# Routing by expert number, a two-column table ahead of the first gathers, and the last scatters behind the branch

## The chip, the cores and the metric

One core of a Trainium2 chip runs the whole program in one launch. The metric is device time in microseconds: 544.03 us is the median of three runs of the kernel before (543.95 to 544.78). The profile is one more execution.

## The reference

Two layers in a row, on 2048 tokens of width 512, all in f32:

```
x  = q                                                   # 2048 x 512
h  = x + q' * (longconv(shift(k) * v) + D * ...)         # q' = layernorm(x)
z  = layernorm(h);  logits = z @ w_gate                  # 8 experts
e  = argmax(logits)  (first on a tie);  gate = softmax over one value
out = h + gate * (silu(z @ w1[e]) @ w2[e])               # F = 1792
```

Each token goes through one expert. The change touches only what lies between the logits and the first expert's first matmul, and the last stores.

## The kernel before

**Stages.** The convolution (a planner, `Plan`, writes each engine's order from costs and due times) fills `h_dram`, 2048 rows of 516 words: 512 of h, then mean, 1/deviation, and the gate in two words. It ends at about 182 us. Then comes the routing, written by hand in program order (L614 to L727), then a branch on `wide_i`, and inside it the experts (`experts(caps)`, L730 to L943), one after another, smallest first.

**Order.** In the routing and the experts every engine runs its instructions in the order in which the program lists them, SP and POOL included; between engines there are only semaphores. An engine that waits holds back all that is listed behind.

**Routing.** A token of partition p and column j (NJ = 16 columns) gets a one-hot row `oh` over experts (L621 to L636) and its place within its expert from a running sum and two matmuls (`incl`, `pn`, `pr`). Experts are ranked by load: `key` (L652), `gt`, `sr` (L657, L660). The place word is rank times 4096 plus place (L668 to L674), cut into column `col_i` and row `lo_f`. The token table, 128 rows by 24 columns (three per expert, in rank order), is a sum of 16 matmuls of one-hot rows `ohlo` (L686, one VectorE instruction per j, 128 x 128) with marked tokens `vt` (L679, L682): `ptab`. From it come `idxg` (gather rows, L694) and `idxs` (scatter rows, L719 to L722).

**First loads.** Two indirect gathers (L707) bring the rows of the first expert's two tiles into `first`; SP loads the first two weight chunks (L715), once it has read the expert's number from `perm_i`. The gathers read `h_dram`, whose last columns are stored by L649. Matmuls `keep_warm` on constants (L605) fill waits on TensorE.

**Branch.** Each engine loads `wide_i` into a register (L947) and branches (L948) to one of three copies of `experts`; these inputs take the copy with the caps SNUG (the first expert has 240 rows, tiles of 128 and 112).

**Experts.** Weights come in 512 KB chunks, 14 per expert (7 for w1, 7 for w2). ScalarE rounds a chunk to `whi`, VectorE takes `wlo = raw - whi` (`split`, L800). Rows are normalised (`norm`, L763), transposed and split into `xh`, `xl` (`turn_x`, L775). `up` (L810) makes 12 matmuls per 128 columns of F, in the order whi.xh, wlo.xh, whi.xl; then ScalarE's Silu (`s`, three buffers), VectorE's `hh`, POOL's `hl`. Loads of chunks 2 to 5 are held back by a write into their tile behind the first `norm` (L797). `store` and `send` (L854) scale by the gate, add h and scatter rows to the output. The last expert's rows leave by three scatters: one of tile 0, two of half-width for tile 1.

## Time and profile before

| | |
|---|---|
| median of 3 runs | 544.03 us |
| the profiled execution | 544.39 us, span 542.5 us |
| TensorE | busy 519.1 us (96%), granted clock 0.991 |
| VectorE, ScalarE, POOL | 75%, 49%, 48% |
| DMA | 105.26 MB, 194 GB/s in the mean |
| convolution, to the last logits | 0 to about 182 us |
| routing, to the first expert matmul | about 182 to 198.6 us |
| experts | 198.6 to about 534.8 us |
| last scatter, landing, end | 534.8 to 542.5 us |

Times below are microseconds from the start of the span. The execution takes 1.9 us more than its span, and lies 0.36 us above the median of the runs.

### The profile page before, as it was taken

What the parts mean: (1) busy time and instruction counts of PE and PEld (TensorE: products, weight loads), DVE (VectorE), ACT (ScalarE), POOL (GpSimd) and SP (SyncE); (2) the same over time, 40 slices, a digit from 0 to 9 for tenths busy, and PEclk for the clock granted to TensorE, in tenths of its full rate; (3) what the DMA queues carried; (4) which work ended last, traced back from release to release, by engine and by line L of the source; (5) the groups of instructions that cost most, each with busy time, mean ns of one, the idle gap of its engine ahead of it and who ended that gap; (6) DMA issues with size and microseconds to landing.
All of it is one profiled execution on the core that took longest, in us unless ns stands there. A gap on an engine that the chain in (4) does not pass through costs nothing. (4 is left out here: it accounts for less than half of the span.)

```text
span 542.5 us, 12152 instructions
## 1 busy us (share of the span) xinstructions
PE 519.1 (96%) x4812; PEld 451.9 (83%) x4812; DVE 405.6 (75%) x558; ACT 265.1 (49%) x410; POOL 260.7 (48%) x297
## 2 busy tenths in 40 slices
PE   9999989999998699999999999999999999999994
PEld 9867767767656469789999999999988988988973
DVE  3779899898997968859855784974884784785851
ACT  2697887544320346545435445545543644554520
POOL 0555659865641136618503921840760760851832
PEclk9999999999999989999999999999999999999998
DMA  8918786659661278674654665674676566576401
GB/s 285 380 55 261 236 276 195 179 153 287 187 170 43 60 263 320 218 256 166 199 182 140 204 199 166 189 259 141 206 219 233 180 210 231 194 219 205 155 2 41
DMA packets 42468, 105.26 MB, mean 194 GB/s; under 512 B 6480, under 2 KB 14800, under 8 KB 42018
## 3 DMA queue, kind: packets, MB, share of 16 engines
q1 hardware_dynamic: 39602, 95.89, 54.9%
q0 software_dynamic: 2800, 8.51, 4.9%
q8 instruction: 40, 0.66, 0.5%
q14 instruction: 26, 0.21, 0.1%
HBM read 95.96 MB, written 8.47 MB: 193 GB/s over the span
## 5 line engine op out<-in xcount | busy, mean ns | idle before, releaser
L826 POOL TENSOR_TENSOR hl<-s,hh 128x240 fp32r<-128x240 f32 (+5 forms) x112 | 114.4, 1035 | 162.2 <-DVE hh L825 161.7
L807 DVE TENSOR_TENSOR wlo<-raw,whi 128x1024 fp32r<-128x1024 f32 x112 | 160.5, 1443 | 38.8 <-ACT whi L806 35.2
L806 ACT ACTIVATE whi<-raw 128x1024 fp32r<-128x1024 f32 x112 | 114.6, 1051 | 3.5 <-DMA raw<-in_w_dram 3.5
L824 ACT ACTIVATE s<-acc 128x240 f32<-128x240 f32 (+5 forms) x112 | 43.1, 387 | 98.1 <-PE acc L821 63.4
L825 DVE CAST hh<-s 128x240 fp32r<-128x240 f32 (+5 forms) x112 | 55.0, 501 | 30.1 <-ACT s L824 29.9
L821 PE MATMUL acc<-xh,whi 128*128 128x240 f32 (+5 forms) x448 | 73.0, 285 | 0.1
L821 PE MATMUL acc<-xh,wlo 128*128 128x240 f32 (+5 forms) x448 | 72.0, 283 | 0.0
L821 PE MATMUL acc<-xl,whi 128*128 128x240 f32 (+5 forms) x448 | 71.9, 283 | 0.0
L821 PEld LDWEIGHTS acc<-xh,whi 128*128 128x128 f32 x448 | 61.7, 189 | 0.8 <-ACT xh L782 0.3
L821 PEld LDWEIGHTS acc<-xl,whi 128*128 128x128 f32 x448 | 61.6, 189 | 0.0
L821 PEld LDWEIGHTS acc<-xh,wlo 128*128 128x128 f32 x448 | 61.4, 189 | 0.0
L842 PE MATMUL acc<-whi,hh 128*128 128x512 f32 (+2 forms) x136 | 54.3, 399 | 0.0
L842 PE MATMUL acc<-whi,hl 128*128 128x512 f32 (+2 forms) x136 | 53.6, 394 | 0.0
L842 PE MATMUL acc<-wlo,hh 128*128 128x512 f32 (+2 forms) x136 | 53.5, 394 | 0.0
L265 POOL TENSOR_TENSOR acc<-acc,ac 128x512 f32<-128x512 f32 x26 | 33.1, 1280 | 37.1 <-ACT acc L253 19.2
L845 PE MATMUL acc<-hh,whi 128*128 128x304 f32 (+2 forms) x168 | 49.8, 296 | 0.0
L845 PE MATMUL acc<-hl,whi 128*128 128x304 f32 (+2 forms) x168 | 49.2, 293 | 0.0
L845 PE MATMUL acc<-hh,wlo 128*128 128x304 f32 (+2 forms) x168 | 49.1, 292 | 0.0
L296 ACT ACTIVATE st<-pa 128x512 f32<-128x512 f32 x64 | 37.3, 595 | 20.6 <-PE pa L293 20.3
L293 PEld LDWEIGHTS pa<-kv,tw 128*128 128x128 f32 x256 | 30.2, 191 | 12.2 <-ACT st L296 8.7
L293 PE MATMUL pa<-kv,tw 128*128 128x128 f32 x256 | 33.5, 282 | 2.2 <-ACT st L296 2.2
L782 ACT ACTIVATE xh<-pt 128x512 fp32r<-128x512 f32 (+5 forms) x18 | 9.6, 535 | 53.1 <-PE pt L781 53.1
(171 smaller groups left out, 878.2 us busy)
## 6 DMA issues: line engine op xcount, KB each, us to landing
raw<-in_w_dram SPq DMA_DIRECT2D x112, 512.0 KB
tv<-in_tab_v_dram SPq DMA_DIRECT2D x12, 512.0 KB
h<-in_q_dram SPq DMA_DIRECT2D x16, 256.0 KB
kt<-in_kt_dram SPq DMA_DIRECT2D x3, 1216.0 KB
v<-in_v_dram SPq DMA_DIRECT2D x12, 256.0 KB
kern<-in_ssm_dram SPq DMA_DIRECT2D x12, 256.0 KB
h<-in_x_dram SPq DMA_DIRECT2D x12, 256.0 KB
h_dram<-h SPq DMA_DIRECT2D x12, 256.0 KB
```

The costliest lines, as they stand in the source:

```text
L265: nc.gpsimd.tensor_add(T[a, c, u], T[a, c, u], T[b, c, u])
L293: nc.tensor.matmul(p[:, :, j], tw[:, u * UJ + j, r, :], src[:, j, :], start=True, stop=True)
L296: nc.scalar.activation(T["s" + kind, c][:, r * NU + u], T["pa", kind, c, u, r], AF.Copy)
L782: nc.scalar.activation(xh[:, at, r0:r0 + m], pt[:, :, :m], AF.Copy)
L806: nc.scalar.activation(whi, raw, AF.Copy)
L807: nc.vector.tensor_sub(wlo, raw, whi.bitcast(F32))
L821: nc.tensor.matmul(pu, a[:, k, fs], b[:, k, :], start=i == 0, stop=i == 3 * ND - 1)
L824: nc.scalar.activation(s, pu, AF.Silu)
L825: nc.vector.tensor_copy(hh[:, f, :], s)
L826: nc.gpsimd.tensor_sub(hl[:, f, :], s, hh[:, f, :].bitcast(F32))
L842: nc.tensor.matmul(pd[:ds_.stop - ds_.start], b[:, f, ds_], a[:, f % 2, :], start=f == 0 and i == 0, stop=f == last - 1 and i == 2)
L845: nc.tensor.matmul(pd, a[:, f % 2, ds_], b[:, f, :], start=f == 0 and i == 0, stop=f == 2 * NCH - 1 and i == 2)
```

## The change

In the routing, places are counted by expert number, not by rank: a constant matmul adds 32 x 128 times the expert (`base_b`, made early on POOL) to `pr`. The place words, tables and one-hots become 16-bit integers or f16 with j innermost. The least loaded expert is found as the minimum of `key` (`least`); two columns (`m0`, `ptab0`, `idx0`) are made for it alone ahead of all else, with the one-hots in two instructions (j 0 to 8, 9 to 15) in place of 16. Then follow the branch flags, the table of 24 columns (`m24`), the ranking, and `perm_i`; the reordering of the table by rank (`other_tables`) goes behind the branch.

The store of mean and 1/deviation is issued behind the reciprocal, with zeros for the gate; the gate (`gated`) is stored later, by SP behind the load of chunk 5, and the first expert's rows are gathered a second time for their gate, in the up stage. `least` in place of `perm_i` gives SP the first expert.

In the first expert both first chunks are rounded ahead of the norms, `wlo` of chunk 0 comes in two halves, and the two column groups of chunk 0 take turns by factor. The last expert's three results are written to tiles `ends`, and the three scatters stand behind the join of the branches.

```
+    sb("kt", "places")                    # 16-bit tables in the buffer of kt, which now stays
...
+    nc.gpsimd.tensor_scalar(base_b, const("e")...[P, E, NJ], 32.0, None, op0=ALU.mult)
+    nc.gpsimd.tensor_copy(tile_b, const("tile")...[P, 24, NJ])
+    nc.gpsimd.tensor_copy(iota_b, const("iota")...[P, P, NJ])
...
+    nc.tensor.matmul(pr, one_b, base_b, start=True, stop=False)
-    keep_warm(5, 128)
+    keep_warm(8, 128)
...
-    nc.vector.reciprocal(rec[:, :, 1], rec[:, :, 1])
     nc.vector.scalar_tensor_tensor(cand, ...)
+    nc.vector.reciprocal(rec[:, :, 1], rec[:, :, 1])
+    nc.sync.dma_start(h_rows[:, :, D:RW], rec)
...
-    keep_warm(5, 128)
-    nc.vector.reciprocal(rec[:, :, 2], rec[:, :, 3])
-    nc.gpsimd.tensor_mul(rec[:, :, 2], rec[:, :, 2], rec[:, :, 3])
-    nc.sync.dma_start(h_rows[:, :, D:RW], rec)
+    keep_warm(8, 128)
     nc.vector.scalar_tensor_tensor(key, pn, float(E), const("e"), ...)
+    nc.vector.tensor_reduce(least, key, axis=AX.X, op=ALU.min)
+    nc.vector.tensor_scalar(least, least, E - 1, None, op0=ALU.bitwise_and)
+    for t in range(2):
+        nc.gpsimd.tensor_scalar(tile0[:, t], least.to_broadcast([P, NJ]), 32.0, float(t), ...)
...
+    r2, c_i, col_i, lo_i                  # 4 VectorE instructions; lo_i is a bitwise and
+    m0 = marks("m0", tile0, 2)            # is_equal, then times tok_b: 128 x 32 each
+    for js in (range(0, 9), range(9, NJ)):
+        nc.vector.tensor_tensor(ohlo[:, :, at], iota_b[:, :, at], lo_i[:, at]..., op=ALU.is_equal)
+        for j in js:
+            nc.tensor.matmul(ptab0, ohlo[:, :, j], m0[:, :, j], ...)
+    keep_warm(2, 512)
+    nc.vector.tensor_scalar(idx0, ptab0, -1.0, 0.0, op0=ALU.add, op1=ALU.max)
+    over, nover, nover, wide_i            # as before, now behind idx0
+    m24 = marks("m24", tile_b, 24)        # 128 x 384 each
+    for j in range(NJ):
+        nc.tensor.matmul(ptab, ohlo[:, :, j], m24[:, :, j], ...)
+    keep_warm(2, 448)                     # before: keep_warm(4, 432)
+    nc.scalar.activation(tabs_e..., ptab, AF.Copy)
     gt, sr, eqm, eqe, perm_i              # moved here, all on VectorE
+    nc.vector.reciprocal(gated[:, :, 0], gated[:, :, 1])
     for t in range(2):
         nc.gpsimd.indirect_dma_start(out=rows0[t], ..., in_offset=... idx0[:, t:t + 1])
+    nc.gpsimd.tensor_mul(gated[:, :, 0], gated[:, :, 0], gated[:, :, 1])
-    place0 = nc.sync.value_load(perm_i[0:1, ORDER[0]:ORDER[0] + 1], ...)
+    place0 = nc.sync.value_load(least[0:1], ...)
...
+    def other_tables():                   # 3 VectorE, then 6 small POOL instructions
...
+        for s in range(len(raw0)):
             load_w(s)
+            split_hi(s)                   # whi of chunks 0 and 1
+        norm(0, *firsts[0])
+        split_lo(0, 0, 512)
         for s in range(len(raw0), AHEAD):
             load_w(s, s < 6)
+            if s == 5:
+                nc.sync.dma_start(h_rows[:, :, D + 2:RW], gated)
+        norm(0, *last, 0); norm(0, *last, 1); split_lo(0, 512, 1024)
+        turn_x of all tiles; split_lo(1); other_tables(); split(2); split(3)
...
+                for fs in ([0, 1],) if s == 0 else ([2 * r], [2 * r + 1]):
+                    up(n, fs, whi, wlo)
+                if n == 0 and 2 <= r < 2 + len(tiles(0)):
+                    gather(0, r - 2)
...
+    scatter(out, idxs[:, end - 1:end], ends[0], S)       # behind the Else arm
+    for i in range(2):
+        scatter(halves, half_i[:, i:i + 1], ends[i + 1], 2 * S)
```

## Rows read from the trace of the kernel before

**Rows 1.** Busy time by stage (window; its length; busy us and count of TensorE's matmuls, its weight loads, VectorE, ScalarE, POOL; granted clock; DMA share; GB/s).

```profile
187.00:200.00 13.00, 9.95 (x43) 6.04 (x44) 8.99 (x37) 3.77 (x9) 5.43 (x9) 0.74 0.65 185
...
260.00:500.00 240.00, 240.00 (x1738) 227.38 (x1738) 167.56 (x194) 114.85 (x180) 106.20 (x102) 1.00 0.62 200
```

**Rows 2.** VectorE in order of time, in the routing (start, duration of the merged group, engine, line, operation, output and input, count).

```profile
183.48 0.26 DVE L627 RECIPROCAL rec<-rec 128x16 f32<-128x16 f32 x1
183.65 0.23 DVE L629 SCALAR_TENSOR_TENSOR cand<-eq,cs 128x128 f32<-128x128 f32 x1
...
185.33 0.17 DVE L652 SCALAR_TENSOR_TENSOR key<-pn,cs 128x8 f32<-128x8 f32 x1
...
187.52 0.55 DVE L679 TENSOR_TENSOR ohhi<-tile_b,col_i 128x384 f16<-128x384 bf16 x1
187.99 3.32 DVE L686 TENSOR_SCALAR ohlo_f<-iota_b,lo_f 128x128 f16<-128x128 f16 x16
191.22 0.27 DVE L691 TENSOR_TENSOR over<-key,rungs 1x128 f32<-1x128 f32 x1
...
191.73 0.16 DVE L694 TENSOR_SCALAR idxg<-pt 128x24 int32<-128x24 f32 x1
...
192.04 0.16 DVE L697 TENSOR_REDUCE wide_i<-nover 1x2 int32<-1x16 f32 x1
```

**Rows 3.** SP's queue and POOL in order of time: the store of the last columns of `h_dram`, the first weight loads, the first two gathers.

```profile
185.61 0.61 SPq L649 DMA_DIRECT2D h_dram<-rec  x1
188.62 0.94 SPq L715 DMA_DIRECT2D raw<-in_w_dram  x2
...
192.20 1.20 POOL L707 DMA_INDIRECT first<-h_dram,idxg  x1 [3.22 <-DVE wide_i L697]
193.71 0.95 POOL L707 DMA_INDIRECT first<-h_dram,idxg  x1 [0.30 <-issue]
```

**Rows 4.** POOL's sequencer on the line of the gathers: four waits for DMA queues, from the first, which ends when the store of L649 has landed, to the last (duration min/median/max in ns, then first and last start).

```profile
L707 POOLq EVENT_SEMAPHORE  x4: 17/43/43, 190.8 to 191.1; - x4
```

**Rows 5.** From the branch to the first expert matmul: the register loads ahead of the branch on VectorE and ScalarE, then ScalarE, VectorE and TensorE in order of time.

```profile
L947 ACTq TENSOR_LOAD <-wide_i x1: 466/466/466, 192.2 to 192.2; - x1
...
193.52 1.06 ACT L806 ACTIVATE whi<-raw 128x1024 fp32r<-128x1024 f32 x1 [1.40 <-DMA raw<-in_w_dram]
197.17 0.60 ACT L782 ACTIVATE xh<-pt 128x512 fp32r<-128x512 f32 x1 [2.59 <-PE pt L781]
198.15 0.69 ACT L782 ACTIVATE xh<-acc 128x224 fp32r<-128x224 f32 x2 [0.38 <-PE acc L781]
...
195.82 0.55 DVE L772 TENSOR_SCALAR xr<-first 128x512 f32<-128x512 f32 x1
...
197.24 0.74 DVE L772 TENSOR_SCALAR xr<-first 112x256 f32<-112x256 f32 x2 [0.84 <-DMA first<-h_dram,idxg]
...
198.56 0.82 PE L821 MATMUL acc<-xh,whi 128*128 128x240 f32 x4
```

**Rows 6.** TensorE in order of time (matmuls of the tables and of `keep_warm`), and last the stretch in which its granted clock was at half (columns as in rows 1).

```profile
182.50 1.48 PE L607 MATMUL warm<-cs 128*128 128x128 f32 x10
...
189.03 2.53 PE L687 MATMUL pt<-vt,ohlo_f 128*128 128x24 f16 x16 [2.25 <-DVE ohlo_f L686]
191.41 4.77 PE L607 MATMUL warm<-cs 128*128 128x432 f32 x8
...
187.87:194.70 6.83, 5.67 (x21) 3.37 (x22) 4.29 (x23) 1.25 (x2) 2.99 (x3) 0.50 0.57 170
```

**Rows 7.** VectorE's groups by line and form between 182 and 200 us (count, busy us, mean ns of one): two inputs of f32 at 1024 and 512 elements per partition, one input at 512 and 256.

```profile
L807 DVE TENSOR_TENSOR wlo<-raw,whi 128x1024 fp32r<-128x1024 f32 x2 | 2.5, 1225 | 3.0 <-ACT whi L806 3.0
L772 DVE TENSOR_SCALAR xr<-first 112x256 f32<-112x256 f32 x2 | 0.7, 410 | 0.8 <-DMA first<-h_dram,idxg 0.8
...
L783 DVE TENSOR_TENSOR xl<-pt,xh 128x512 fp32r<-128x512 f32 x1 | 0.7, 682 | 0.0
...
L772 DVE TENSOR_SCALAR xr<-first 128x512 f32<-128x512 f32 x1 | 0.5, 546 | 0.0
```

**Rows 8.** POOL in the up stage of the first expert, and ScalarE's Silu that waits for it.

```profile
214.42 2.35 POOL L826 TENSOR_TENSOR hl<-s,hh 128x240 fp32r<-128x240 f32 x2 [0.23 <-DVE hh L825]
216.94 1.08 POOL L759 DMA_INDIRECT hr<-h_dram,idxg  x1 [0.17 <-issue]
...
215.16 0.37 ACT L824 ACTIVATE s<-acc 128x240 f32<-128x240 f32 x1 [0.55 <-POOL hl L826]
...
217.62 0.40 PE L842 MATMUL acc<-whi,hh 128*128 128x512 f32 x1
```

**Rows 9.** The end: POOL's last work in order of time, its branch out of the arm, and the drains of POOL and of SP at the end (ns min/median/max, first and last start).

```profile
518.21 2.35 POOL L826 TENSOR_TENSOR hl<-s,hh 128x240 fp32r<-128x240 f32 x2 [0.22 <-DVE hh L825]
533.03 1.00 POOL L857 DMA_INDIRECT out_dram<-o,idxs  x1 [12.47 <-DVE o L856]
...
535.61 0.95 POOL L857 DMA_INDIRECT out_dram<-o,half_i  x1 [0.30 <-POOLq L948]
...
L948 POOLq COMPARE_BRANCH  x1: 46/46/46, 535.4 to 535.4; - x1
...
L1119 POOLq DRAIN  x1: 3311/3311/3311, 538.3 to 538.3; - x1
...
L1119 SPq DRAIN  x2: 7/10/13, 540.4 to 540.5; - x2
```

More of the change, by code (lines that the diff above doesn't have):

```diff
@@ L153 @@
     oh = keep.tile([P, E, NJ], BF16, name="oh")
-    tile_b = keep.tile([P, 24], BF16, name="tile_b")
     tok_b = keep.tile([P, NJ], F16, name="tok_b")
-    c_i = keep.tile([P, NJ], I32, name="c_i")
-    col_i = keep.tile([P, NJ], I32, name="col_i")
-    lo_f = keep.tile([P, NJ], F32, name="lo_f")
+    gated = keep.tile([P, NJ, 2], F32, name="gated")
+    c_i = keep.tile([P, NJ], I16, name="c_i")
+    col_i = keep.tile([P, NJ], I16, name="col_i")
+    lo_i = keep.tile([P, NJ], I16, name="lo_i")
     perm_i = keep.tile([1, E], I32, name="perm_i")
@@ L164 @@
     idxs = keep.tile([P, 24], I32, name="idxs")
-    iota_b = keep.tile([P, P], F16, name="iota_b")
+    idx0 = keep.tile([P, 2], I32, name="idx0")
     tri_b = keep.tile([P, P], BF16, name="tri_b")
@@ L435, in casts @@
             nc.gpsimd.tensor_scalar_add(rungs[:, 0, i], rungs[:, 1, i], 8.0 * (SNUG[i] - TIGHT[i]))
-        for a, n in ((iota_b, "iota"), (tri_b, "tri"), (one_b, "one"), (tile_b, "tile")):
+        for a, n in ((tri_b, "tri"), (one_b, "one")):
             nc.gpsimd.tensor_copy(a, const(n))
@@ L598 @@
     plan.run(PACE, ZERO, AHEAD)
+    sb("kt", "places")
+    place_f = T["places"].rearrange("p a b -> p (a b)")
+    place_h = place_f.bitcast(I16)
+    iota_b = place_h[:, :P * NJ].rearrange("p (m j) -> p m j", j=NJ)
+    tile_b = place_h[:, P * NJ:(P + 24) * NJ].rearrange("p (c j) -> p c j", j=NJ)
+    tile0 = place_h[:, (P + 24) * NJ:(P + 26) * NJ].rearrange("p (c j) -> p c j", j=NJ)
+    base_b = place_f.bitcast(BF16)[:, (P + 26) * NJ:(P + 26 + E) * NJ].rearrange("p (e j) -> p e j", j=NJ)
+    hr_at = (P + 26 + E) * NJ // 2
+    rows0 = [place_f[:, hr_at + t * RW:hr_at + (t + 1) * RW] for t in range(2)]
+    nc.gpsimd.tensor_scalar(base_b, const("e").unsqueeze(2).to_broadcast([P, E, NJ]), 32.0, None, op0=ALU.mult)
+    nc.gpsimd.tensor_copy(tile_b, const("tile").unsqueeze(2).to_broadcast([P, 24, NJ]))
+    nc.gpsimd.tensor_copy(iota_b, const("iota").unsqueeze(2).to_broadcast([P, P, NJ]))
     conv.close()
@@ L672 @@
         nc.vector.tensor_reduce(perm_i, eqe, axis=AX.X, op=ALU.add)
-    with nc.allow_low_precision(reason="whole numbers under 32768"):
-        nc.vector.tensor_reduce(c_i, by_j(r2), axis=AX.X, op=ALU.add)
-    nc.vector.tensor_scalar(col_i, c_i, 7, None, op0=ALU.logical_shift_right)
-    nc.vector.scalar_tensor_tensor(lo_f, col_i, -float(P), c_i, op0=ALU.mult, op1=ALU.add)
-    ohhi = small([NJ, 24], "ohhi", F16)
-    nc.vector.tensor_tensor(ohhi, tile_b.unsqueeze(1).to_broadcast([P, NJ, 24]), bc(col_i, 24),
-                            op=ALU.is_equal)
@@ L681 @@
-    vt = small([NJ, 24], "vt", F16)
-    nc.gpsimd.tensor_tensor(vt, ohhi, bc(tok_b, 24), op=ALU.mult)
-    ohlo = ohlo_f.bitcast(F16).rearrange("p (j m) -> p j m", j=NJ)
-    ptab = ps_t.tile([P, 24], F32, name="pt")
-    for j in range(NJ):
-        nc.vector.tensor_scalar(ohlo[:, j, :], iota_b, lo_f[:, j:j + 1], None, op0=ALU.is_equal)
-        nc.tensor.matmul(ptab, ohlo[:, j, :], vt[:, j], start=j == 0, stop=j == NJ - 1)
-    keep_warm(4, 432)
-    over = small([2, E, E], "over", parts=1)
```

209 lines of the change are left out of this document (122 added, 87 removed).

## Prediction

> **What bounds the kernel now.** First the busy time by stage. Among the experts TensorE is busy all of the time at the full granted clock (240.00 of 240.00 us); in the routing it has 9.95 of 13 us, at a granted clock of 0.74, and most of that is `keep_warm` [rows 1]. So behind 198.56, where the first expert matmul starts, every us is TensorE's and the change takes no matmul away; before it there is a chain of small steps on which TensorE waits. What the first matmul gains, the end gains, as long as weights keep up.
>
> Then the chain itself, in the order of time. VectorE goes without a gap from `key` at 185.33 over eleven instructions to the first `ohlo` at 187.99, makes sixteen `ohlo` in 3.32 us, and has the gather rows, `idxg`, at 191.73 [rows 2]. POOL issues the first gather at 192.20, the second at 193.71 [rows 3]. The second tile is read at 197.24, 3.53 us behind its issue, and 1.32 us later the first matmul starts [rows 5]. The gather also had to wait for the store of L649: issued at 185.61, it had landed at 190.8, 5.2 us later, and three more waits took POOL to 191.1 [rows 3, 4]. That was 0.8 us early enough; it is what comes up next if `idxg` comes sooner.
>
> At the end the last scatter starts at 535.61; POOL's branch out of the arm is at 535.4, its drain starts only at 538.3, lasts 3.31 us, and SP's drain, which waits for the landing, is at 540.4 [rows 9]. The 542.5 of the span follows POOL's drain.
>
> **The change, part by part.** All times are in the clock of the trace before.
>
> *Up to the places.* The reciprocal goes behind `cand`, which takes its place, 183.65 - 183.48 = 0.17 us sooner [rows 2]. From `key` (now 185.16) to the first `ohlo` there were eleven instructions in 2.66 us, `ohhi` alone 0.47 of it, so 0.22 for each of the other ten [rows 2]. Nine remain (`key`, two for `least`, `r2`, `c_i`, `col_i`, `lo_i`, two for `m0`): 1.97 us, first `ohlo` at 187.13. `base_b`, `tile_b`, `iota_b` are made on POOL while it has nothing to do in the last 16 us before the routing, and `tile0` beside `r2`; I cost them at nothing. Without that cover the two of `tile0` would cost about 0.3 each.
>
> *The one-hots.* Two instructions of 1152 and 896 elements per partition replace sixteen of 128. The trace has no two-input instruction with only two-byte operands. Two f32 inputs cost (1225 - 682)/512 = 1.06 ns per element, one input (546 - 410)/256 = 0.53 [rows 7]. These are the two ends: with 0.1 us between them and the fixed part of the last, 1.45 us or 2.41 us, so an end at 188.58 or 189.54, against 191.31 before [rows 2]. I take 0.53: the one-input rows show that VectorE passes two elements per cycle when its ports carry them, and the new operands bring half the bytes per element of those that ran at 1.06; `ohhi` (0.55 us at 384 elements) is no counter-example, since one of its inputs has four bytes [rows 2].
> The Trainium skill, in "VectorE: DVE Perf Modes", section "The perf-mode tier table (the rule you actually need)", gives two-input instructions double rate in SBUF on two-byte data and single rate on f32. By it the one-hots end at 188.58; by the nearest two-input row they end at 189.54 and the whole gain falls to 1.2 us. No run here shows it yet.
>
> *The index.* Before, `idxg` came 0.42 us behind the last `ohlo`, with one matmul left; now seven are left. Six more at between 0.05 and 0.16 us (the sixteen of before took 2.53, held by VectorE [rows 6]); I take 0.4. `idx0` at 189.4, done at 189.56, against 191.89.
>
> *The store.* It is issued behind the reciprocal, at 183.9 in place of 185.61, and with the same 5.2 us and the waits behind it frees POOL at 189.4 [rows 3, 4]. So it stays just off the chain. The gate's store, 2048 small pieces more, goes on SP behind chunk 5; chunks 6 and 7 wait 0.6 us behind it, and TensorE needs them over 15 us later.
>
> *The gathers.* 0.31 behind `idx0` as before: 189.87 and 191.38, 2.33 us sooner; the second tile is there at 194.9. The two weight loads leave about 1.1 us sooner (`least` in place of `perm_i`), so they still overlap; 0 to 0.6 us, taken as 0.2 and off the chain, as follows.
>
> *What now stands ahead of the branch.* VectorE: flags 0.9, `m24` 0.6 (1.0 at 1.06 ns), ranking to `gated` six at 0.22, so the branch at 192.2; before it took 1.3 us from the register load at 192.2 to the first work behind it on ScalarE, at 193.52 [rows 5]. First norm at 193.5 (before 195.82). TensorE: `ptab0` ends at 189.3, then four instructions of `keep_warm` with 512 columns. 128 columns cost (1.48 - 0.28)/9 = 0.13 us each at the full clock, 432 columns 0.6 mostly at half [rows 6]: 2.1 us at full, 2.9 at half. I take full, because the longer `keep_warm` of the change fills the wait in which the clock fell before (half from 187.87 to 194.70 [rows 6]). Then sixteen matmuls for `ptab`, 0.8 to 2.6 us, taken as 1.0: 192.4. ScalarE copies `tabs_e` (0.2), branches (1.3), and rounds both chunks ahead of `xh`: 193.9, 194.9, `xh` at 196.0, and the first matmul 0.6 + 0.35 later [rows 5]: 196.95. By the gathers alone it would be 194.9 + 1.32 = 196.2. **So ScalarE, held by the second table, is late next**, and the start gains 198.56 - 196.9 = 1.7 us.
>
> *Second gather of the first expert, on POOL.* Two more at 1.08 + 0.17 us. POOL has no pause in this stage, and `s` waits for `hl` [rows 8]. `hl` 6 and 7 come 1.25 us later, `s` 9 with them at 216.4, while the down stage needs its PSUM tile at 218.3, behind its first matmul at 217.62 [rows 8]; the later `hl` have over 5 us. Hidden, with about 1.5 us to spare; without that cover up to 1.0 us. `other_tables` is under 1 us of VectorE between chunks 1 and 2, whose `wlo` has 1 us and more; hidden. Turning the two column groups of chunk 0 by factor only moves the need for `wlo` and `xl` later.
>
> *The end.* POOL's last `hl` ends at 520.6, 12.47 us before its first scatter [rows 9], so POOL jumps to the join in that pause and the scatters wait there. Each still starts when its result is there (at most 0.1 us sooner). What goes is the 2.9 us between branch and drain: the drain starts at about 536.6. If its 3.31 us are its own, SP's at 540.4 ends the kernel, 1.15 us sooner; if it waits for the scatters, nothing is gained. I take the middle, 0.6.
>
> **Sum**: 1.7 + 0.6 = 2.3 us. On the profiled execution 544.39 - 2.3 = 542.1; on the median of the runs 541.7.
>
> **The rivals.**
>
> *VectorE stays at 1.06 ns.* For: the nearest two-input row. Then `idx0` is 1.0 later, `m24` 0.4 more, and the start gains 0.6: 542.8.
>
> *The clock falls all the same.* For: it fell before in the routing, behind a wait of 2.25 us [rows 6]; waits of up to 1 us remain ahead of each group of `ptab0`. Then `keep_warm` costs 0.75 and `ptab` 0.8 more in front of `tabs_e`, start gains 0.15: 543.3; more if it lasts into the expert.
>
> *The join holds the scatters (slower).* If POOL's scatters are released not by each result but by VectorE's arrival behind its own branch, 2.9 us after its last result as POOL's own jump shows, the first starts near 538.0 and the third 2 x 1.29 later, at 540.6 instead of 535.6 [rows 9]: 5 us later, 1.7 gained, 547.3. It decides from the point at which the first scatter starts more than 1.5 us behind its result. Against: at the start, POOL's gathers follow the one result they read by 0.31 us.
>
> *The start doesn't move*, because the gathers and the two weight loads, now at the same time, slow each other, or the store lands later: 543.4 to 544.
>
> **How the numbers follow.** The forecast 0.60, VectorE's rate 0.15, the clock 0.12, the join 0.07, no move 0.06. Two runs differ from no change at about 0.2%, 1.09 us: faster is below 542.94, slower above 545.12. Faster: 0.58 of the forecast, 0.10 of the rate, 0.04 of the clock, 0.72. Slower: 0.07 and 0.01 of the clock, 0.08. Same: 0.20. The forecast's own bounds are start 1.5 to 2.4 and end 0 to 1.2, so 540.4 to 542.5. To hold 8 in 10 the range takes in the rate and a part of the clock: 540.2 to 543.5.
>
> **What would show it.** Right: two `ohlo` of about 0.7 and 0.6 us; `idx0` by 189.6; gathers at about 189.9; ScalarE's first `whi` behind `tabs_e` and the first `xh` behind both `whi`; first expert matmul at 196.5 to 197; full TensorE from there on, also around the start of the first down stage; three scatters 0.3 us behind their results and a drain that starts by 537. Wrong: `ohlo` of 1.2 us; half clock across 190 to 195; scatters in a row behind the last result; a hole in TensorE near 218.

## The result, and the profile after

The kernel after takes 547.82 us (547.21 to 548.97 over six runs) against 544.01 us for the kernel before on the same chip: ratio 1.0071, 95% interval 1.0058 to 1.0084. It is slower by 0.7%, where 541.7 was forecast. The profiled execution took 547.72 us, its span 545.59, 3.12 us more than the 542.47 of before. Of the runs below, one of the kernel "the same, more warming" (634.65 us) and one of "end inside the arms" (853.5 us) were slow and are left out of the medians. The two spans, cut where the named instructions start:

| stretch | before, us | after, us | difference |
|---|---|---|---|
| start to the maximum `mx` (convolution) | 182.77 | 181.72 | -1.05 |
| `mx` to first expert matmul | 15.79 | 15.06 | -0.73 |
| chunk 0 of the first expert | 2.90 | 4.01 | +1.11 |
| rest of its up stage | 16.16 | 16.16 | 0 |
| its down stage | 20.90 | 24.75 | +3.85 |
| second expert to the first matmul of the last tile's halves | 293.28 | 293.29 | 0 |
| from there to the end | 10.67 | 10.60 | -0.07 |

The first line is not the change's: over all profiles below it lies between 181.6 and 183.4 us, whichever routing follows. So 4.96 us were lost in chunk 0 and the first down stage, two stretches in which the forecast had expected nothing.

Busy time by stage, of before (chunk 0, rest of the up stage, down stage of the first expert) and then of after (columns as in [rows 1], which the first and last line of after answer to):

```profile
198.56:201.46 2.90, 2.90 (x24) 2.87 (x25) 2.33 (x5) 2.29 (x3) 0.00 (x0) 1.00 0.93 339
201.46:217.62 16.16, 16.16 (x146) 16.16 (x145) 13.75 (x18) 10.28 (x18) 9.28 (x9) 1.00 0.87 318
217.62:238.52 20.90, 20.90 (x98) 16.27 (x97) 18.20 (x20) 11.05 (x15) 7.53 (x9) 1.00 0.75 252
```

```profile
187.00:200.00 13.00, 10.43 (x66) 7.50 (x66) 8.97 (x31) 4.79 (x8) 3.07 (x6) 0.87 0.77 238
196.78:200.79 4.01, 4.01 (x25) 4.01 (x26) 3.94 (x8) 2.43 (x3) 0.91 (x2) 0.68 0.91 339
200.79:216.95 16.16, 16.16 (x147) 16.16 (x146) 11.19 (x17) 8.03 (x17) 10.38 (x14) 1.00 0.94 296
216.95:241.70 24.75, 22.70 (x98) 17.27 (x97) 18.82 (x21) 12.15 (x17) 9.53 (x11) 0.93 0.72 231
195.94:199.35 3.41, 3.38 (x16) 2.92 (x16) 3.38 (x7) 1.77 (x3) 0.00 (x0) 0.50 0.90 336
230.07:233.49 3.42, 3.42 (x9) 2.51 (x8) 3.42 (x5) 1.07 (x2) 0.00 (x0) 0.50 0.80 266
260.00:500.00 240.00, 240.00 (x1732) 227.38 (x1731) 169.86 (x196) 115.17 (x180) 110.45 (x103) 1.00 0.62 201
```

Two stretches now run at half the granted clock (1.2 GHz): one in chunk 0, and one behind a pause of TensorE in the down stage. In that down stage TensorE idles for 2.05 us of the 24.75.

**The start.** VectorE in the order of time, answering to [rows 2]:

```profile
184.12 0.17 DVE L666 SCALAR_TENSOR_TENSOR key<-pn,cs 128x8 f32<-128x8 f32 x1 [0.27 <-PE pn L660]
185.89 1.52 DVE L695 TENSOR_TENSOR ohlo_f<-kt,lo_i 128x1152 f16<-128x1152 int16 x2
188.10 0.16 DVE L700 TENSOR_SCALAR idx<-pt 128x2 int32<-128x2 f32 x1 [0.70 <-PE pt L698]
189.07 0.34 DVE L686 TENSOR_TENSOR m<-kt,col_i 128x384 f16<-128x384 int16 x1
```

From `key` to the index 3.98 us, before 6.40. Then SP's store, POOL's gathers, and the waits of POOL's sequencer ahead of them (the lines answer to [rows 3], the last to [rows 4]):

```profile
182.86 0.60 SPq L648 DMA_DIRECT2D h_dram<-rec  x1
189.47 1.19 POOL L734 DMA_INDIRECT kt<-h_dram,idx  x1 [4.34 <-DVE m L686]
190.96 0.95 POOL L734 DMA_INDIRECT kt<-h_dram,idx  x1 [0.30 <-issue]
L734 POOLq EVENT_SEMAPHORE  x4: 17/43/43, 188.3 to 188.6; - x4
```

The index starts at 188.10, the gather only at 189.47. From there to the first matmul (answers to [rows 5]):

```profile
192.01 2.00 ACT L846 ACTIVATE whi<-raw 128x1024 fp32r<-128x1024 f32 x2 [0.74 <-DMA raw<-in_w_dram]
194.54 0.60 ACT L825 ACTIVATE xh<-pt 128x512 fp32r<-128x512 f32 x1 [0.52 <-PE pt L824]
193.18 0.55 DVE L815 TENSOR_SCALAR xr<-kt 128x512 f32<-128x512 f32 x1 [2.03 <-DMA kt<-h_dram,idx]
195.32 0.41 DVE L815 TENSOR_SCALAR xr<-kt 112x256 f32<-112x256 f32 x1 [0.96 <-DMA kt<-h_dram,idx]
196.78 2.06 PE L869 MATMUL acc<-xh,whi 128*128 128x240 f32 x8
```

Both norms wait for their gather, so the gathers still set the start. The rows of the second are read 4.36 us behind its issue (3.53 before).

**The hole.** POOL, ScalarE, VectorE and TensorE around it (POOL's and ScalarE's lines answer to [rows 8]):

```profile
217.31 0.94 POOL L802 DMA_INDIRECT hr<-h_dram,idxg  x1 [0.16 <-issue]
218.55 1.36 POOL L802 DMA_INDIRECT hr<-h_dram,idxg  x1 [0.30 <-issue]
219.92 1.38 POOL L874 TENSOR_TENSOR hl<-s,hh 128x240 fp32r<-128x240 f32 x2
220.68 0.37 ACT L872 ACTIVATE s<-acc 128x240 f32<-128x240 f32 x1 [2.62 <-POOL hl L874]
221.09 0.37 DVE L873 CAST hh<-s 128x240 fp32r<-128x240 f32 x1 [1.83 <-ACT s L872]
228.31 0.53 DVE L815 TENSOR_SCALAR xr<-hr 128x512 f32<-128x512 f32 x1
226.46 0.40 PE L890 MATMUL acc<-wlo,hh 128*112 128x512 f32 x1
228.90 0.66 PE L824 MATMUL pt<-cs,xr 128*128 128x128 f32 x4 [2.05 <-DVE xr L815]
```

Read it from below. TensorE waits 2.05 us, from 226.85 on, in the middle of its down stage, to transpose the second expert's rows. The `xr` it waits for (`norm`, L815) stands on VectorE behind the `hh` and `wlo` of the first expert; `hh` waits for `s`, `s` for `hl` to free one of its three buffers, and `hl` stands behind two gathers in a row, the second of the new ones and the first of the second expert's. Before, the same norm was done at 227.06, 0.29 us ahead of the transposes, which start at 227.35 without a wait:

```profile
226.53 0.54 DVE L772 TENSOR_SCALAR xr<-hr 128x512 f32<-128x512 f32 x1
227.35 0.60 PE L781 MATMUL pt<-cs,xr 128*128 128x128 f32 x4
```

**SP behind the gate's store**, and **the end** (answers to [rows 9]):

```profile
197.15 0.55 SPq L944 DMA_DIRECT2D h_dram<-gated  x1
197.97 5.22 SPq L841 DMA_DIRECT2D raw<-in_w_dram  x1
...
536.22 1.00 POOL L757 DMA_INDIRECT out_dram<-end,idxs  x1 [12.41 <-DVE end L905]
537.53 0.98 POOL L757 DMA_INDIRECT out_dram<-end,half_i  x1 [0.30 <-issue]
538.81 0.97 POOL L757 DMA_INDIRECT out_dram<-end,half_i  x1 [0.30 <-DVE end L905]
...
L1181 POOLq DRAIN  x3: 46/107/6182, 538.5 to 545.3; - x3
...
L1181 SPq DRAIN  x3: 7/7/13, 543.7 to 545.0; - x3
```

The load that follows the gate's store takes 5.22 us to issue; its neighbours take 0.33. ScalarE, which rounds the chunks, then waits longer for a load; its waits between 205 and 230 us of before and of after (total, times, longest):

```profile
ACT whi L806 <- DMA raw<-in_w_dram: 1.0, 1, 1.0
ACT whi L846 <- DMA raw<-in_w_dram: 3.2, 2, 2.3
```

At the end each scatter follows its result by 0.3 to 0.4 us, and POOL's drain starts 3.0 us sooner against the last scatter than before, but lasts 6.18 us instead of 3.31.

### The profile page after: what moved, and what is told of

It reads as the page before. It is cut to its first block, busy times and chain, and to the rows that moved or that the text cites. A ratio compares the mean times of both kernels' runs of the same rounds, so it can differ in the third digit from the quotient of the medians.

```text
span 545.6 us, 12214 instructions
## 1 busy us (share of the span) xinstructions
PE 521.6 (96%) x4841; PEld 454.6 (83%) x4841; DVE 403.8 (74%) x553; ACT 264.8 (49%) x410; POOL 266.2 (49%) x303
## 4 chain that ended last, share of the span: by engine, by line
PE 53%; issue 2%; POOL 1%; POOLq 0%; DVE 0%; DVEq 0%
PE acc L869 26%; PE acc L890 13%; PE acc L893 12%; PE pt L824 1%; PE pt L913 1%; POOL out_dram L757 0%; POOL hl L874 0%; POOLq L1181 0%; DVE hh L873 0%; POOLq L757 0%; DVEq L851 0%; POOLq L1001 0%
## 5 line engine op out<-in xcount | busy, mean ns | idle before, releaser
L874 POOL TENSOR_TENSOR hl<-s,hh 128x240 fp32r<-128x240 f32 (+5 forms) x112 | 116.0, 1048 | 156.7 <-DVE hh L873 156.1
L851 DVE TENSOR_TENSOR wlo<-raw,whi 128x1024 fp32r<-128x1024 f32 (+1 forms) x113 | 158.5, 1413 | 39.6 <-ACT whi L846 35.6
L267 POOL TENSOR_TENSOR acc<-acc,ac 128x512 f32<-128x512 f32 x26 | 33.1, 1280 | 36.4 <-ACT acc L255 18.4
```

What stands on the lines that cost most here:

```text
L267: nc.gpsimd.tensor_add(T[a, c, u], T[a, c, u], T[b, c, u])
L851: nc.vector.tensor_sub(wlo[:, a:b], RAW[s][:, a:b], whi[:, a:b].bitcast(F32))
L874: nc.gpsimd.tensor_sub(hl[:, f, :], s, hh[:, f, :].bitcast(F32))
```

## The experiments

Each was timed beside the kernel before on its own chip; the ratios are to that. First all of them in one table, since one quantity orders them: the time from the first `whi` on ScalarE to the norm of the second expert on VectorE (**chain**). "Hole" is the time from the start of the last matmul ahead of TensorE's transposes of the second expert to the first of these; 0.23 is one matmul, that is no hole. The run whose pause lies elsewhere, the second expert's gathers ahead of chunk 0, is left to its place. Each line's chain and hole come from one profiled execution, which is not always near the median: that of "late second gather" and of "after, own tile, four `s`" is the fastest of its runs, that of "the same, more warming", of "after, more warming", of "after, no gate store" and of "chunk 0 whole" the slowest.

| kernel | chain, us | hole, us | down stage, us | median, us | ratio, 95% interval |
|---|---|---|---|---|---|
| before | 33.0 | 0.24 | 20.90 | 544.0 | 1 |
| after | 36.3 | 2.44 | 24.75 | 547.82 | 1.0058 to 1.0084 |
| late second gather | 32.9 | 0.24 | 20.93 | 543.22 | 0.9971 to 0.9997 |
| before, two gathers more | 33.8 | 0.91 | 21.63 | 545.38 | 1.0016 to 1.0042 |
| late gather, own table tile | 32.5 | 1.50 | 22.26 | 543.80 | 0.9978 to 1.0003 |
| the same, more warming | 34.0 | 1.59 | 22.39 | 543.60 | 0.9972 to 1.0000 |
| second gather first | 35.0 | 1.88 | 22.60 | 545.43 | 1.0016 to 1.0034 |
| end inside the arms | 32.5 | 1.43 | 22.16 | 544.09 | 0.9988 to 1.0010 |
| after, four `s` | 33.1 | 0.23 | 20.93 | 543.37 | 0.9970 to 0.9996 |
| late gather, own tile, four `s` | 30.1 | 0.23 | 20.87 | 542.42 | 0.9955 to 0.9976 |
| before, four `s` | 29.1 | 0.24 | 20.91 | 544.12 | 0.9993 to 1.0011 |
| after, own tile, four `s` | 32.7 | 1.32 | 22.05 | 543.85 | 0.9986 to 1.0003 |
| after, own tile | 36.2 | 3.05 | 24.83 | 547.37 | 1.0034 to 1.0067 |
| after, more warming | 35.8 | 3.07 | 26.19 | 545.47 | 1.0014 to 1.0054 |
| after, no gate store | 34.6 | 3.07 | 26.00 | 544.83 | 0.9992 to 1.0026 |
| after, gate store behind loads | 33.7 | 2.69 | 23.48 | 544.28 | 0.9991 to 1.0021 |
| late gather, own tile, four `s`, chunk 0 whole | 29.2 | 0.23 | 20.90 | 541.90 | 0.9942 to 0.9974 |
| late gather, gate behind loads | 32.0 | 0.24 | 20.91 | 542.95 | 0.9953 to 0.9986 |

**The second gather of the first expert in the down stage** (from after):

```diff
-                hr = X["hr", n, t] = xp.tile([P, RW], F32, name=f"hr{t}")
+                hr = X["hr", n, t] = xp.tile([P, RW], F32, name=f"hr{t}") if n else rows0[t]
...
-                if n == 0 and 2 <= r < 2 + len(tiles(0)):
-                    gather(0, r - 2)
...
                 down(n, 2 * r + 1, whi, wlo)
+                if n == 0 and 4 <= r < 4 + len(tiles(0)):
+                    gather(0, r - 4)
```

> The changed kernel with one thing moved: the second gather of the first expert's rows leaves the up stage and goes behind the fifth and sixth chunk of its down stage, into the tiles that held the rows first. Theory (POOL's queue): in the changed kernel these two gathers stand between the hl of the first expert, hold back s, and with it VectorE, whose norm of the second expert comes 2 us late for TensorE's transposes at 226.9; the pause then brings half clock from 230.07 to 233.49. Without them the down stage of the first expert takes 20.9 us as before, not 24.75: 547.8 - 3.8 = 544.0 us (543.5 to 544.6). Rival (the reordering of the table behind the branch delays POOL's first hl, and that is the hole): the down stage stays at 24 us or more, 547 to 548 us.

The gathers now also write into the tiles of the first reading, and not into new ones. 543.22 us, 4.6 less than after, as the theory had it. In the profile the down stage has no hole, at the full clock throughout:

```profile
195.40:199.91 4.51, 4.51 (x25) 4.49 (x26) 4.36 (x9) 1.70 (x3) 1.28 (x2) 0.62 0.93 307
215.99:236.92 20.93, 20.93 (x98) 16.30 (x97) 18.18 (x20) 11.06 (x15) 10.48 (x10) 1.00 0.83 281
```

So the loss goes with the two gathers' place. And the half clock in chunk 0, still there (4.51 us), is not it. It even hides what is left: the norm is done only 0.37 us ahead of the transposes here, and the runs with the late gather and chunk 0 at the full clock have a hole of 1.4 to 1.6 us (below).

**Two such gathers put into the kernel before** (its `gather(0)` out of the up stage's front, and in the loop as in after):

```diff
+                if n == 0 and 2 <= r < 2 + len(tiles(0)):
+                    gather(0, r - 2)
```

> The kernel before with one thing added: the first expert's rows are gathered a second time in its up stage, at the places of the change. Theory (POOL's queue): the down stage of the first expert grows from 20.9 us by 2 to 4 us, with a pause of TensorE ahead of the first transposes of the second expert: 546.0 to 548.0 us. Rival (the gathers are hidden, as predicted): 544.0 us, no pause.

545.38: slower, but by 1.4 us, under a third of what moving them gave, and the down stage grows by 0.7 us where 2 to 4 were expected. The pause is there (0.91), so the rival is out, and the theory's size was too large. Something else in the change makes the gathers dearer; four runs further below look for it.

**A tile of its own for the table**, on top of the late gather (the kernel after keeps `tile_b` in the tile into which the first gathers write; POOL's copy into it moves with it, into the routing):

```diff
-    tile_b = place_h[:, P * NJ:(P + 24) * NJ].rearrange("p (c j) -> p c j", j=NJ)
+    tile_b = ctx.enter_context(tc.tile_pool(name="tbp", bufs=1)).tile([P, 24, NJ], I16, name="tile_b")
```

> As e1_late_regather, and the table of column numbers for the 24 columns has a tile of its own. Theory: in the changed kernel the first gather starts 1.2 us behind idx0 and not 0.3, because its destination lies in the same tile as the table that m24 reads, so that it waits for m24. With its own tile the gather starts 0.3 us behind idx0 or as the store of the row statistics has landed (188.4), and the first expert matmul comes 0.9 us sooner: 543.1 us, 0.9 below e1_late_regather. Rival (it waits for the landing of that store): same start and same time as e1_late_regather.

**More keep_warm** ahead of the first expert, on top of that:

```diff
-    keep_warm(2, 448)
+    keep_warm(3, 448)
...
             turn_x(0, *a)
+            nc.tensor.matmul(ps_u.tile([P, 512], F32, name="acc"), const("one"), cs[:, :512], start=True, stop=True)
```

> As e3_own_table_tile, with more matmuls on constants: three of 448 columns ahead of the branch and not two, and one of 512 columns between the transposes of the first and of the second tile. Theory: the first chunk takes 4.0 us in the changed kernel and not 2.7, because the granted clock is at half from 195.94 to 199.35 behind two pauses of TensorE of 1.2 and 1.3 us; with the pauses filled the clock stays full and the first chunk takes 2.7 us: 1.3 us below e3_own_table_tile, 541.8 us. Rival (the chunk waits for wlo or xl): no change of the first chunk; or the added matmuls hold the transposes: up to 0.5 us more.

Chunk 0 ran at the full clock in both (2.90 and 2.82 us), and neither is faster than the run with the late gather alone: what chunk 0 saves comes back as a hole of 1.5 and 1.6 us. TensorE reaches its transposes sooner, the norm it needs does not come sooner.

That the shared tile held the first gather is refuted. The run with the end inside the arms (below) has the shared tile, and its gather starts 0.47 us behind the start of the index and ahead of the table's `m` (190.81):

```profile
L734 POOLq EVENT_SEMAPHORE  x4: 17/43/43, 188.0 to 188.2; - x4
...
189.84 0.16 DVE L700 TENSOR_SCALAR idx<-pt 128x2 int32<-128x2 f32 x1 [0.70 <-PE pt L698]
...
190.31 1.20 POOL L734 DMA_INDIRECT kt<-h_dram,idx  x1 [3.42 <-DVE over L703]
190.81 0.34 DVE L686 TENSOR_TENSOR m<-kt,col_i 128x384 f16<-128x384 int16 x1
```

What does hold it is the store's landing. In the eight profiles where the gather starts later than 0.47 us behind the start of the index, it starts 0.85 to 0.86 us behind the end of POOL's last wait for the store and the queues (after: 188.61 to 189.47); in the others that wait had ended earlier. The releaser that the trace names there, VectorE's `m`, was only the last to finish by the profile. The tile of its own saves three of the four queue waits, 0.26 us.

**The second gather ahead of chunk 0** (from after):

```diff
-                if n == 0 and 2 <= r < 2 + len(tiles(0)):
-                    gather(0, r - 2)
...
             split(s)
+        for a in tiles(0):
+            gather(0, a[0])
         for s in range(2 * NCH * E):
```

> After, with the second gather of the first expert's rows kept in the up stage but put ahead of its first chunk, where POOL has nothing else, instead of behind chunks 2 and 3. Theory (the two gathers cost by standing between the hl subtractions on POOL, which s on ScalarE waits for): down stage of the first expert 20.9 to 21.5 us instead of 24.75, no TensorE hole near 226 us, time 543.0 to 544.5. Rival (the second reading costs by its transfer or by its tiles, wherever it is issued): 546.5 to 548. Rival (it waits for the gate's store, some 202 us, and holds the first hl there): first hl later than 205 us and 544.5 to 546.5.

**The second expert's gathers ahead of chunk 0**, on top of the run with the tile of its own:

```diff
+        for a in tiles(1):
+            gather(1, a[0])
...
-                if 3 <= r and n + 1 < E:
+                if n and 3 <= r and n + 1 < E:
```

> The earlier run with the late second gather and the table tile of its own, and in addition the second expert's three gathers put ahead of the first chunk instead of behind chunks 3 to 5. Theory (what is left of the hole, 1.5 us at 226, is the same chain: gathers between the hl subtractions, then s, then the next expert's norm): s waits for hl less, down stage 20.9 to 21.3 us instead of 22.3, first expert matmul still some 14 us behind mx, time 542.0 to 543.0, ratio to before about 0.997. Rival (the chain of weights, from the load over whi and wlo to the norm, sets it, without POOL): down stage stays 22 to 22.5 us and the time 543.5 to 544.

Both theories missed; the last rival of the first run is what came. POOL is not free there: the first gather reads `h_dram` and so waits for the gate's store. That wait ends at 206.4, 8.0 us behind the store's issue at 198.4, and the gather starts at 207.15. POOL's line of the first run, TensorE's of the second:

```profile
207.15 1.11 POOL L802 DMA_INDIRECT hr<-h_dram,idxg  x1 [3.63 <-DMA h_dram<-gated]
...
211.71 1.21 PE L869 MATMUL acc<-xh,whi 128*128 128x240 f32 x4 [3.01 <-ACT s L872]
```

The first took 545.43 us. The second took 545.40 (ratio 1.0017 to 1.0042): `hl` begins only at 210.55, `s` runs out of buffers, TensorE out of PSUM, and it waits 3.01 us, up to 211.71. The same chain, hit earlier. In this profile its granted clock is at half from 210.74, within that wait, to 217.57.

**The last scatters back inside the arms**, on top of the late gather:

```diff
         store(E - 1, *first_rows, ends[0])
+        scatter(out, idxs[:, end - 1:end], ends[0], S)
         store_by_halves(E - 1, *last_rows)
+        for i in range(2):
+            scatter(halves, half_i[:, i:i + 1], ends[i + 1], 2 * S)
...
-    scatter(out, idxs[:, end - 1:end], ends[0], S)
-    for i in range(2):
-        scatter(halves, half_i[:, i:i + 1], ends[i + 1], 2 * S)
```

> The earlier run with the late second gather, with the last three scatters back inside each arm as before the change. Theory (the end's gain was small because POOL's drain ends with the landing of the last scatter, not with the branch): last matmul to the end of the span 6.8 to 7.2 us against 7.5 there, wholly by the landing, time 543.2 to 543.5. Rival (the branch in front of the drain costs what was forecast): end longer by 0.6 us and 543.8.

The theory missed, and the rival came near: the expectation leaned on the single pair before and after. From the start of the last held matmul to the end of the span this run takes 8.30 us; the four profiles with the scatters inside take 7.86 to 8.30, mean 8.05, the fifteen with them outside 6.88 to 7.89, mean 7.39. So the move is worth some 0.66 us on average, and the kernel after (7.88) was at the slow end of its kind. The drains tell why. Inside the arms POOL's drain starts late and lasts 3.31 to 3.48 us in all four, here too, where SP's drain, behind the landing, is over 2.6 us ahead of its end; so these are its own. Outside, it ends about 1.06 us behind SP's drain in every profile: it follows the landing. The 544.09 against 543.22 also holds a hole of 1.43, which the scatters can't make; chunk 0 ran at the full clock in this profile.

**Four buffers of s instead of three**, in after, and in the kernel before:

```diff
-            s = xp.tile([P, cap], F32, name="s", bufs=3)
+            s = xp.tile([P, cap], F32, name="s", bufs=4)
```

> After, with four buffers of s instead of three, and the two gathers left where they are. Theory (POOL's lateness reaches the norm over the ring of s, so that one buffer more lets ScalarE and VectorE run ahead by one hl of 0.7 to 1.7 us): waits of s for hl fall from 8.2 us to 4 to 6, the norm of the second expert comes 0.7 to 1.7 us earlier, down stage 22.5 to 24, time 545.5 to 547. Rival (POOL's own late hl hold the down matmuls, not the ring): down stage and time as in after, 547.5 to 548.

> The kernel before with four buffers of s instead of three, nothing else. Theory (the three buffers were enough before, with no gather of the first expert's rows on POOL in its up stage): down stage 20.7 to 21.0 us, time 543.7 to 544.2, ratio 0.999 to 1.0005. Rival (the fourth buffer gains by itself, and what it brought to the kernel after was not the change's loss): 542.5 or less.

In after it takes away 4.4 us, about all of what the late gather takes away and more than the theory expected, though the gathers stay where they are; in the kernel before it changes nothing (544.12). So the ring of three is how POOL's lateness gets to ScalarE and VectorE. Down stage of after with four:

```profile
216.68:237.61 20.93, 20.93 (x99) 16.26 (x97) 17.21 (x19) 11.55 (x16) 9.67 (x12) 1.00 0.76 258
```

**Four buffers and the tile of its own, with the gathers late, and with the gathers in place** (a finished tile's space, `eq`, is used again for `r2` to make room):

> The run with the late second gather and the table tile of its own, and in addition four buffers of s. Theory (with the ring longer, the next expert's norm no longer trails POOL, so that the hole of 1.5 us at 226 goes and the earlier first matmul is kept): first expert matmul 13.9 to 14.2 us behind mx (before 15.8), down stage 20.9 to 21.4 us, time 541.5 to 542.6, ratio to before 0.995 to 0.997. Rival (the chain from the first whi to that norm takes its 33 us whatever s has, and gives the gain back): hole of 1 us or more, 543.2 to 544.

> After with two repairs alone: the table tile of its own (so that the first gather needn't wait for the last read of the table) and four buffers of s; the two second gathers stay in the up stage. Theory: first expert matmul 14 us behind mx and chunk 0 in 2.9 us, but the norm of the second expert still comes some 33 us behind the first whi, so that a hole of 1 to 1.6 us at 226 is left: 542.8 to 543.8. Rival (four buffers give all the slack that is wanted): no hole, 541.5 to 542.4.

Both about as expected: with the gathers late 542.42 us, no hole; with the gathers in place a hole of 1.32 us and 543.85, no different from before. Over the pairs of the table that differ in this alone a fourth buffer takes 2.5 to 4 us off the chain, and the gathers add 2.6 to 3.7 us to it in the new kernel and 0.8 in the old.

**Chunk 0 not split**, on top of the first of these two:

```diff
-                for fs in ([0, 1],) if s == 0 else ([2 * r], [2 * r + 1]):
+                for fs in ([2 * r], [2 * r + 1]):
...
-        split_lo(0, 0, 512)
...
-        split_lo(0, 512, 1024)
+        split_lo(0)
```

> The run with the late second gather, the table tile of its own and four buffers of s, with the change's splitting of the first chunk undone: its wlo in one operation behind the norms, and its two column blocks one after the other instead of interleaved. Theory (with the first chunk at the full granted clock the split hides at most the half of one wlo, 0.5 to 0.6 us, and the chain behind it sets the end of the stage): first expert matmul as before the undoing, chunk 0 in 3.0 to 3.6 us instead of 2.9, time 542.3 to 542.9. Rival (the split is what carries the earlier start): chunk 0 of 4 us or more, 543.4 or more.

541.90 us (five runs), ratio 0.9942 to 0.9974: the best of all, though by no more than the interval, and a little below what was expected. Chunk 0 takes 3.32 instead of 2.89 us, and the whole up stage 19.48 instead of 19.42, so the split has no measurable worth here.

**Why the gathers cost more in after: the clock or the store?** The tile of its own alone, and more warming alone, both from after:

> After with the table tile of its own alone: three buffers of s, the two second gathers where they are. In the trace of after, TensorE stood 1 us further behind the first whi when chunk 1 began (8.8 us) than in the kernel before with two gathers (7.8 us), by half clock in chunk 0. Theory (that lateness delays s too, and adds to what the gathers cost): if chunk 0 runs at full clock here, chunk 1 begins 6 to 7 us behind the first whi, the norm of the second expert some 34 us behind it, the down stage takes 22 to 23.2 us, time 544.3 to 546. Rival (the gathers cost the 3.4 us of the chain by themselves, whatever the clock in chunk 0): norm 36 us behind the first whi, down stage 24 us or more, 547 to 548.

> After with more keep_warm alone (three instead of two behind the second table, and one behind each transposed tile of the first expert): the tables, the gathers and s as they are. Theory (as in the run with the table tile alone): where chunk 0 runs at full clock, down stage 22 to 23.5 us and 544.5 to 546.3. Rival (the gathers by themselves): down stage 24 us or more and 547 to 548.

Chunk 0 ran at the full clock in both profiles (2.90, 2.82 us), and the chain still took 36.2 and 35.8 us. The first run, profiled near its median, came out as the rival had it, 547.37: the half clock in chunk 0 doesn't multiply the gathers. The second leaves it open by its time: its median, 545.47, lies in the theory's range, and its profile is the slowest of seven runs (544.70 to 548.88). Then the gate's store on SP, left out (so that the experts' results are missing from the sum), and moved:

```diff
-            if s == 5:
-                nc.sync.dma_start(h_rows[:, :, D + 2:RW], gated)
+        nc.sync.dma_start(h_rows[:, :, D + 2:RW], gated)
         for a in firsts[1:]:
             norm(0, *a)
```

> After without the later store of the gate (2048 pieces of 8 bytes, issued by SP behind the load of chunk 5), so that the gate read by the second gathers is zero and the experts' results are left out of the sum; the two second gathers stay. In the trace of after the next load on SP, that of chunk 6, takes 5.2 us to issue instead of 0.33. Theory (that blocked load, and not the gathers alone, makes the difference to the kernel before with two gathers): load of chunk 7 issued some 6 to 7 us behind the first whi instead of 11.5, norm of the second expert 33.5 to 34.5 us behind the first whi instead of 36.3, down stage 21.5 to 23 us, time 544 to 546. Rival (SP is ahead anyway, and the gathers alone cost it): norm 36 us behind the first whi, down stage 24 us or more, 547 to 548.

> After with the same store of the gate moved behind the load of chunk 7 on SP, nothing else. Theory (it blocks the loads of chunks 6 and 7, which ScalarE comes to first): these two are issued at once, the block falls on the load of chunk 8, which waits for its buffer until about 12 us behind the first whi anyway; norm of the second expert 33.5 to 35 us behind the first whi, down stage 21.5 to 23.5 us, time 544 to 546.3. Rival: as after, 547 to 548.

3.0 and 3.5 us less than after, both in the theory's range. The loads of chunks 6 and 7 then issue one behind the other (198.45 and 199.05 without the store), in after at 197.97 and 203.46. With the store moved the blocked load is that of chunk 8: SP's loads between 190 and 216 us, min, median and longest in ns, of after and of this run:

```profile
L841 SPq DMA_DIRECT2D raw<-in_w_dram x13: 332/333/5225, 194.4 to 215.9; - x13
L841 SPq DMA_DIRECT2D raw<-in_w_dram x13: 332/333/6656, 195.6 to 215.1; - x13
```

The block is there and costs less: that load is issued by 208.08, and ScalarE comes to its chunk at 212.24. The holes did not shrink with the chain, because TensorE comes sooner too. In thirteen of the sixteen profiles with the new routing its first expert matmul starts 3.05 to 3.56 us behind the first `whi` (in after itself 4.77), in the three with the old 4.89 to 5.04, and the norm does not follow. So chains that differ by 0.8 us, without the store (34.6) and in before with two gathers (33.8), give holes of 3.07 and 0.91. The profiled execution without the store is its slowest run (547.35, median 544.83), so its down stage of 26.0 us isn't typical; the hole in it is followed by a half clock from 229.55 to 232.97, as in after, and the moved store's hole of 2.69 us is not. That may be part of the spread of these runs (542.94 to 547.35); one profile of each can't show it.

**Both moved**, the late gather and the gate's store behind the loads, with three buffers:

> After with both moved and nothing else: the second gathers of the first expert in the down stage, the gate's store behind the load of chunk 7. Three buffers of s, the tables as they are. Theory (the loss is these two together, and without them the change brings what it saves at the start and the end, some 1.6 and 0.6 us): norm of the second expert 31 to 32.5 us behind the first whi, no TensorE wait of over 0.3 us ahead of its transposes, down stage 20.9 to 21.3 us, time 541.6 to 542.7, ratio 0.9955 to 0.9975. Rival (the chain still has no slack, as in the run with the late second gather alone): a hole of 0.5 to 1.5 us, 542.9 to 543.8.

542.95, ratio 0.9953 to 0.9986; no hole, down stage 20.91. The median is 0.25 us above what was expected, the ratio inside it. Against the late gather alone, with chunk 0 at half clock in both profiles, the chain is 0.9 us shorter: that is what moving the store adds. The norm is done 1.70 us ahead of the transposes instead of 0.37, in part because TensorE began 1.0 us later behind the first `whi`.

## Why the prediction was wrong, point by point

**The step that failed** is "Second gather of the first expert, on POOL", with its verdict "Hidden, with about 1.5 us to spare". It followed the later `hl` to one user only, the PSUM tile, and looked for a hole near 218; the hole came at 226.85. The other user is the ring of `s`: behind `s` stand, in program order, `whi` on ScalarE, `hh` and `wlo` on VectorE, and behind these the norm of the second expert, which TensorE wants in the middle of the down stage. Before, that norm was done 0.29 us ahead of the transposes; in after and wherever TensorE waited for it, they start 0.06 us behind it, so 0.23 us were to spare. In after the norm came 3.3 us later behind the first `whi`, and the transposes were due 0.8 us later (chunk 0 took longer): 3.3 - 0.8 - 0.2 gives the 2.2 us by which TensorE came late. The other 1.6 of the 3.85 us lost in the down stage go with the half clock behind the hole. That it is the gathers and the ring is shown thrice: by moving the gathers, by lengthening the ring, and by a control that the ring alone gains nothing.

**A second term failed beside it**: the gate's store. "Chunks 6 and 7 wait 0.6 us behind it" counted its issue (0.55 us) and not what it does to the next DMA: 5.22 us, so that chunk 7 leaves 11.5 us behind the first `whi` instead of 6.3. Over all profiles with this store the DMA behind it took 4.6 to 6.7 us to issue; the median of the loads is 0.33. The Trainium skill, "Perfetto Trace Analysis", section "DMA Instruction — HWDGE (DVE, Sync)", says that a DMA keeps the descriptor generator locked until its descriptors are all made. The trace agrees in part only: the next DMA is held, but the store's own issue, in which the page puts the making of its descriptors, took 0.55 us. With the gathers the store makes the chain 36 us; either alone leaves 32.9 to 34.6. Neither was among the rivals, and the slower rival that was named, the join, is refuted: each scatter is 0.3 to 0.4 us behind its result. Its 547.3 comes near the measured time by chance.

**VectorE's rate: right.** 1.52 us for the two `ohlo` against 1.45 forecast and 2.41 by the nearest row of before. The rule of the Trainium skill ("VectorE: DVE Perf Modes", "The perf-mode tier table (the rule you actually need)") agrees with that number. The rival is out.

**The start: right in size, wrong in its bound.** Forecast 1.7 us, held by ScalarE behind the second table. `mx` to first matmul took 15.79 to 15.84 in the three profiles with the old routing and 13.70 to 15.06, mean 14.31, in the sixteen with the new: 1.5 us gained on average, 0.73 in the profiled execution of after. But `xh` waits for the transposes, these for the norm and that for the gather, so the size came out right in part by luck. "It stays just off the chain", said of the store, failed: the store took 5.4 us, not 5.2, and 0.86 us pass between POOL's last wait and the gather. Counted with these 0.86 us the store was 0.2 us off the chain before, not the "0.8 us early enough" of the prediction. And the second gather's rows were there 4.36 us behind its issue, where 3.53 had been carried over.

**The clock.** It did not fall in the routing after 187 as before, but in chunk 0 (195.94 to 199.35), at a cost of 1.1 us there; the rival had the right event and the wrong place. It costs little in the end: where the chain is late anyway, a faster chunk 0 is handed back as a hole. The second fall, behind the hole, was in no term.

**The end: right in size.** 0.6 forecast between 0 and 1.15; 0.66 on average. Both cases that were named are true, each in its place: begun late, the drain's 3.3 us are its own; begun early, it waits for the landing. That the middle taken between them came out is luck, since neither case gives it.

**The sum.** 1.5 + 0.66 = 2.2 us is what the change does bring, against 2.3 forecast, and the three kernels without the chain's loss get 1.4, 1.9 and 2.2 of it against the kernel before on their chips (542.95, 542.42, 541.90). In these three the norm is done 1.5 to 2.0 us ahead of the transposes. Two more have no hole in their profiles, late gather and after with four `s`, but there the norm is only 0.4 and 0.9 us ahead, with chunk 0 at half clock; they get 0.8 and 0.7 us. The forecast was wrong by what it called hidden.

**Open**: when TensorE's clock falls. It fell in chunk 0 in the profiles of after, late gather, four `s`, and both moved, not in the others. In these four TensorE had paused twice between 192 us and its first expert matmul, 0.64 to 1.46 us each (1.24 and 1.29 in after); in the other twelve with the new routing it paused there at most once, for up to 1.21 us (pauses under 0.35 us are not counted). That is what goes with the fall; that it makes it is not shown. Behind the later hole the pause's length doesn't tell: see the last point below. And how much each of the two causes costs alone in the finished kernel is known only from runs in which other things moved with them.

## What to carry to other kernels

"Hidden" has to be followed to every reader of the late buffer, and past it to what stands behind that reader on its engine, up to the engine that sets the time; the slack is that of the tightest one, here 0.2 us. A ring that is just long enough is a coupling: one buffer more was worth 4.4 us here, and nothing in the kernel without the disturbance. A small DMA of many pieces can hold the next DMA on its queue, as the gate's store did, and is better placed where that one is not wanted soon. It need not: behind the store of `rec`, 2048 pieces too, the next load came 3.0 us later and took 0.38 us to issue. What makes the difference was not tested.

## What the hardware showed that was not expected

- A store of 2048 pieces issued in 0.55 us and held the next load on SP for 4.6 to 6.7 us; POOL's wait for its landing ended 8.0 us behind its issue.
- POOL's drain behind the scatters costs 3.3 to 3.5 us by itself when it begins 2.6 to 2.9 us behind the start of the last scatter, and ends 1.06 us behind SP's drain when it begins right there.
- A hole of 2.44 us in TensorE was followed by 3.42 us at half clock in one profile (after), holes of 2.69 and 3.05 us by none in two others (gate store behind loads, own tile).
